# Lightning attention and a low-rank mixer on one core: low-rank rows through ScalarE, V converted a step sooner, and 64x64 score tiles from step nine

## The chip, the cores and the metric

The kernel runs on one core of a Trainium2 chip. The metric is the time of one execution in microseconds on the device. Eight runs of the kernel before took 674.75 to 678.09 us, with a median of 675.93. Five engines work side by side: TensorE (PE; its weight loads are listed apart as PEld), VectorE (DVE), ScalarE (ACT), GpSimd (POOL), and SyncE (SP), which only issues DMAs here. Matrix products land in PSUM, which VectorE and ScalarE read; everything else lies in SBUF.

## What is computed

The first half is attention with a decay per head, in 4 batches, 8 heads, 768 positions and head size 64. The second half mixes the positions through a rank of 32 and the channels through a layer of 2048:

```python
intra = np.einsum('bhic,bhjc->bhij', qb, kb) * Dmask[None]      # scores, masked by lam ** (i - j)
intra = np.einsum('bhij,bhjd->bhid', intra, vb)
inter = np.einsum('bhid,bhde->bhie', qb * lam_pow[None], kv_state)
out[:, :, sl] = intra + inter
kv_state = lam_block[None, :, None, None] * kv_state + np.einsum('bhsd,bhse->bhde', kb_dec, vb)
...
h = xt @ U @ V                                                   # xt: positions last, rank 32
u = x + h.transpose(0, 2, 1)
ch = np.maximum(u @ w_ch1, 0.0) @ w_ch2
return (u + ch).astype(np.float32)
```

U, V, w_ch1 and w_ch2 arrive as float64. The kernel reads them as pairs of 32-bit words and makes float32 of them with integer and float operations. The products of the second half run on a reduced float32 format. So an operand is split into a high part (its upper bits, by a mask) and a low part (the rest), and the products of the parts are added.

## The kernel before

**Steps.** The positions are cut into 24 steps of 128 (6 per batch, `NT`), and the first part of the kernel runs through them with an order that is written out by hand (lines 546 to 566; each engine takes its work in just this order). A step s turns q and k of step s+1 (`prep`, L348 on TensorE, copied out by ScalarE, L351), multiplies the masked scores by V (`intra`, L446), copies the result x to SBUF (L451, ScalarE), updates the state (`state`, L411 on TensorE and L417 or L419 on VectorE), makes the scores of the next step (`scores`, L393), multiplies q by the state (`inter`, L434), and masks the scores (`masked`, L402, VectorE). There are nine buffers for x. GpSimd scales k (L365) and q (L376). SyncE issues the loads of q, k and V three to five steps ahead (L272) and waits for buffers to come free in the order of its own queue.

**Scores.** For each of eight heads the scores are a product of k with 64 rows and q. For steps 0 to 11 it is one product with 128 columns of k (form 64x128); from step 12 on it is two products with 64 columns each, into the upper and the lower half of the output (form 64x64). L411, L434 and L446 have 64 output rows per product throughout.

**The low-rank stage.** When a batch's six x are there, `low` (L461) forms the 32 low-rank rows of the batch in PSUM, in four groups of 32 partitions (tile `pp`, in the bank with the tag `pq`, which the next q transposes also use). `low_rows` brings them to SBUF side by side, as 32 rows of 512, split: four VectorE masks out of PSUM (L474) make the high part `p_h`; four VectorE subtractions, also out of PSUM (L480), make the low part. ScalarE spreads the high part to two places (L485, L486) and copies the low part (L489). `next_of_low` issues these pieces in between other work. Then `mix` (L499) multiplies V's split by these rows, VectorE adds the result to x (L502), and `turn` (L516) transposes the sum, splits it (L521 and after) and stores it (L519). This store is what frees a buffer of x. For batches 0 to 2 the stage lies in steps 6, 12 and 18; for batch 3 it lies among the first products of the channel layer (`rest`, L769), where ScalarE also reads the products' results (L720).

**Side work.** The conversion of U, V and the first two tiles of w_ch1 is cut into pieces, which the table at L623 gives to steps; `aside` issues them at the end of a step, and what falls to ScalarE comes in the next step (`late`). V's pieces are two fetches, four pieces of conversion (L154 to L184, with L160 and L161 on ScalarE), the mask and first copies (L597, L604), the low part (L608 on VectorE and on GpSimd).

**After the steps** come the two channel products: `hidden` (L714, L724) makes u times w_ch1 with weights that are converted alongside and stores the result; `product` (L847, L849, L851) multiplies by w_ch2.

Of the kernel before, what the change touches and what calls it, by code (L numbers as in the profile page):

```python
# [10 lines left out]
U32 = mybir.dt.uint32  # L11
AF = mybir.ActivationFunctionType
ALU = mybir.AluOpType

P = 128
# [3 lines left out]
def kernel(  # L19
# [28 lines left out]
    nc = tc.nc  # L48
# [3 lines left out]
    NT = S // P  # L52
# [4 lines left out]
    R = moe_U.shape[1]  # L57
# [6 lines left out]
    HI = 0xFFFFF000  # L64
# [16 lines left out]
    def on_scalar(what):  # L81
        if late and late[0] is None:
            late.append(what)
        else:
            what()
# [12 lines left out]
    def tmp(name):  # L98
        return wconv.tile([P, C], FP32, tag="tmp", bufs=3, name=name)
# [125 lines left out]
    def w1_steps(ft, in_parts=False):  # L225
        def tile_of():
            w1v[ft] = w1_pool.tile([P, 3, C], F32R, tag="w1", name="w1")
            return w1v[ft]

        cols = moe_w_ch1[:, ft * P : (ft + 1) * P].rearrange("(c p) f -> p c f", p=P)  # L230
        return split_steps(tile_of, cols, in_parts)
# [13 lines left out]
    def two_banks(name, tag):  # L245
        return psf.tile([P, 2, N], FP32, tag=tag, name=name)

    def one_bank(shape, name, tag):
        return psf.tile(shape, FP32, tag=tag, name=name)
# [80 lines left out]
    half = [slice(0, D), slice(D, P)]  # L330

    def keep_busy(n):

        out = one_bank([P, C], "idle", "pq")
        for i in range(n):
            nc.tensor.matmul(out=out[:, 0:P], lhsT=blank, rhs=blank, start=True, stop=True)
# [50 lines left out]
    def scores(s):  # L387
        qt, kt = st[s]["qt"], st[s]["kt"]
        st[s]["pss"] = pss = two_banks("pss", "pss").rearrange("p x (a i) -> p x a i", a=HP)
        for a in range(HP):  # L390
            for x in range(2):
                for rows in half if s >= 2 * NT else [slice(0, P)]:
                    nc.tensor.matmul(  # L393
                        out=pss[rows, x, a, :], lhsT=kt[half[x], a, rows],
                        rhs=qt[half[x], a, :], start=True, stop=True,
                    )
# [57 lines left out]
    pps = {}  # L454
# [12 lines left out]

    def low_rows(b):

        pp, t = pps.pop(b), tmp("p_h")[0:R]  # L470
        h, h2, l, l2 = (p_hl[g * R : (g + 1) * R] for g in range(G))
        own = [(slice(g * R, (g + 1) * R), slice(g * P, (g + 1) * P)) for g in range(G)]
        for rows, cols in own:
            nc.vector.tensor_scalar(  # L474
                t[:, cols].bitcast(U32), pp[rows].bitcast(U32), HI, None, ALU.bitwise_and
            )

        def low_part():
            for rows, cols in own:
                nc.vector.tensor_tensor(  # L480
                    out=l[:, cols], in0=pp[rows], in1=t[:, cols], op=ALU.subtract
                )

        def spread():
            nc.scalar.copy(h, t)  # L485
            nc.scalar.copy(h2, t)  # L486

        def spread_low():
            nc.scalar.copy(l2, l.bitcast(FP32))  # L489

        pps[b] = [spread, low_part, spread_low]
# [55 lines left out]
    for s in range(NS):  # L547
        b, c = divmod(s, NT)
# [20 lines left out]
    def load_next(name, engine=nc.sync):  # L569
# [3 lines left out]

    run = {
        "prep": prep, "fade": fade, "scores": scores, "masked": masked, "inter": inter,
        "intra": intra, "state": state,
        "low": low, "low_rows": low_rows, "next_of_low": next_of_low, "mix": mix, "turn": turn,
        "scale": scale, "turned": lambda s: turned.pop(s)(),
    }
    def v_steps():  # L580

        st = {}

        def dst():
            if "v" not in st:
                st["v"] = wconv.tile([P, C], FP32, tag="wf", name="vf")[0 : 2 * R, 0:SH]
            return st["v"]

        def parts(gs):
            for half in range(2):  # L590
                rows, cols = slice(half * R, (half + 1) * R), slice(half * SH, (half + 1) * SH)
                for g in gs:
                    yield v_hl[g * R : (g + 1) * R, cols], rows

        def five():
            st["t"] = t = wconv.tile([P, C], FP32, tag="wt", name="vt")[0 : 2 * R, 0:SH]
            nc.vector.tensor_scalar(  # L597
                t.bitcast(U32), st["v"].bitcast(U32), HI, None, ALU.bitwise_and
            )
            on_scalar(lambda: high(0))  # L600

        def high(g, copy=nc.scalar.copy):
            for out, rows in parts((g,)):
                copy(out, st["t"][rows])  # L604

        def low(g, engine):
            for out, rows in parts((g,)):
                engine.tensor_tensor(  # L608
                    out=out, in0=st["v"][rows], in1=st["t"][rows], op=ALU.subtract
                )  # L610

        halves = [moe_V[:, half * SH : (half + 1) * SH] for half in range(2)]
        return weight_steps(dst, halves, SH, 2 * R, in_parts=True) + [
            five, lambda: low(1, nc.vector), lambda: high(2, nc.vector.tensor_copy),
            lambda: low(3, nc.gpsimd),
        ]
# [5 lines left out]
    side = {}  # L622
    for steps, at in (  # L623
        (u_side, (-1, 1, 1, 2, 2)),
        (v_steps(), (0, 0, 3, 3, 4, 4, 4, 5, 4, 5)),
        (w1_steps(0, True), (3, 4, 5, 6, 8, 9, 10, 11, 12, 13, 14)),
        (w1_steps(1, True), (8, 9, 10, 11, 15, 16, 17, 18, 19, 20, 21)),
    ):
        assert len(steps) == len(at)
        for step, n in zip(steps, at):  # L630
            side.setdefault(n, []).append(step)
# [28 lines left out]
    keep_busy(2)  # L660
    pl = one_bank([P, H], "pl", "pt")
    nc.tensor.matmul(out=pl, lhsT=lam_row[:, H:], rhs=lam_row[:, 0:H], start=True, stop=True)
    keep_busy(3)
    nc.vector.tensor_copy(out=lamb, in_=pl)
    constants()
    powers()
# [101 lines left out]
    c0, b = NS - NT, B - 1  # L768
# [181 lines left out]
```

## Time and profile before

| what | value |
|---|---|
| median of eight runs | 675.93 us (674.75 to 678.09) |
| the profiled execution | 678.09 us, its span 676.1 us |
| mean granted TensorE clock | 1.000 |
| TensorE busy | 666.7 us, 99% of the span |
| VectorE, ScalarE, GpSimd busy | 498.2, 277.5, 113.4 us |
| DMA | 131.27 MB, mean 194 GB/s |
| steps of the first part | from 4.5 to 125 us |
| channel layer | from 125 us to the end |
| L393 in form 64x128, in form 64x64 | 192 matmuls of 296 ns, 384 of 275 ns |
| L474, L480 (VectorE, 32x128) | 16 of 285 ns, 16 of 288 ns |
| L485, L486, L489 (ScalarE, 32x512) | 4 each of 617, 618, 616 ns |

In the timelines a line has the start in us from the beginning of the span, the duration in us, the engine, the line of the kernel, the operation, the tiles written and read, the shape and the count; in square brackets stands how long the engine was idle before, and who ended that. In the chain of waits a line has start, duration, and the engine and line, or the DMA, that the end of the kernel hung on at that time. In the list of groups, "busy, mean ns" are the total time and the mean duration of one instruction. A float32 matmul counts as two in the profile's counts, since the hardware runs it as two passes.

### The profile page before, as it was taken

The page shows a single profiled execution, that of the slowest core. Times are in us where ns is not written, and L with a number is a line of the kernel's source. Part 1 is how long each engine was busy: PE and PEld are TensorE (multiplying, and loading weights), DVE is VectorE, ACT ScalarE, POOL GpSimd, SP SyncE. Part 2 cuts the span into 40 slices and gives each one's busy share as a digit, 9 for nine tenths or more (in the row PEclk, how much of TensorE's full clock was granted, in tenths as well). Part 3 has the DMA queues.
Part 4 walks back from the last instruction along what each step waited for, and adds up shares of the span by engine and source line. Part 5 has one row for each costly group of instructions (what it writes and reads, how often), then busy time and mean ns, then how long its engine had stood idle before and what let it go on. Part 6 is the DMA issues. An engine that isn't in the chain of part 4 may idle for free.

```text
span 676.1 us, 13173 instructions
## 1 busy us (share of the span) xinstructions
PE 666.7 (99%) x5124; PEld 545.1 (81%) x5124; DVE 498.2 (74%) x879; ACT 277.5 (41%) x513; POOL 113.4 (17%) x92
## 2 busy tenths in 40 slices
PE   9998999999999999999999999999999999999997
PEld 7887888887888888888888888888888888888886
DVE  4678989777999777777798255786686776865864
ACT  4665658544555444444455122232232322322320
POOL 4455767331000000000000000030030210300300
PEclk9999999999999999999999999999999999999999
DMA  8888987164777655555667999844363353453431
GB/s 196 207 201 215 236 208 188 56 213 141 255 258 253 234 202 203 202 203 194 211 249 248 329 313 391 303 165 155 104 203 106 113 194 102 148 164 94 157 93 62
DMA packets 131775, 131.27 MB, mean 194 GB/s; under 512 B 81346, under 2 KB 89794, under 8 KB 131714
## 3 DMA queue, kind: packets, MB, share of 16 engines
q1 hardware_dynamic: 130656, 130.18, 61.2%
q8 instruction: 40, 0.66, 0.4%
q10 hardware_dynamic: 1058, 0.26, 0.2%
q14 instruction: 21, 0.17, 0.1%
HBM read 80.09 MB, written 50.33 MB: 193 GB/s over the span
## 4 chain that ended last, share of the span: by engine, by line
PE 94%; ACT 2%; DVE 2%; DMA 2%; issue 0%; DVEq 0%; ACTq 0%
PE pz L714 27%; PE pz L849 13%; PE pd L724 13%; PE pz L847 13%; PE pd L851 13%; PE px L446 3%; PE pss L393 3%; PE put L516 2%; PE pq L348 1%; PE pkv L411 1%; PE px L434 1%; PE pk L348 1%; DMA vraw<-in_v_dram 1%; DMA u_d<-x_nat 1%; PE pp L461 1%; PE pu L499 1%
## 5 line engine op out<-in xcount | busy, mean ns | idle before, releaser
L714 PE MATMUL pz<-u_hl,w 128*128 128x512 f32 x768 | 190.5, 397 | 0.0
L714 PEld LDWEIGHTS pz<-u_hl,w 128*128 128x128 f32 x768 | 144.0, 188 | 35.5 <-issue 0.4
L849 PE MATMUL pz<-w_hl,m 128*128 128x512 f32 x384 | 151.1, 396 | 0.0
L847 PE MATMUL pz<-w_hl,m 128*128 128x512 f32 x384 | 150.9, 396 | 0.0
L851 PE MATMUL pd<-w_d,m 128*128 128x512 f32 x384 | 149.5, 396 | 0.0
L830 ACT ACTIVATE m<-mt 128x512 fp32r<-128x512 f32 x96 | 60.7, 633 | 196.3 <-PE pd L851 130.0
L831 DVE SCALAR_TENSOR_TENSOR m<-rm,m 128x512 fp32r<-128x512 f32 x96 | 71.4, 745 | 45.5 <-ACT m L830 45.3
L876 POOL TENSOR_TENSOR o<-o,u 128x512 f32<-128x512 f32 x20 | 29.8, 1523 | 447.4 <-DVE o L872 447.4
L729 DVE SCALAR_TENSOR_TENSOR r<-pd,r 128x512 f32<-128x512 f32 x96 | 61.8, 686 | 53.6 <-ACT r L720 43.5
L724 PE MATMUL pd<-u_d,w 128*128 128x512 f32 x384 | 98.6, 397 | 0.0
L720 ACT ACTIVATE r<-pz 128x512 f32<-128x512 f32 x96 | 52.2, 596 | 93.4 <-PE pz L714 93.3
L849 PEld LDWEIGHTS pz<-w_hl,m 128*128 128x128 f32 x384 | 72.3, 188 | 17.7
L847 PEld LDWEIGHTS pz<-w_hl,m 128*128 128x128 f32 x384 | 72.3, 188 | 17.6
L851 PEld LDWEIGHTS pd<-w_d,m 128*128 128x128 f32 x384 | 72.3, 188 | 17.6
L724 PEld LDWEIGHTS pd<-u_d,w 128*128 128x128 f32 x384 | 72.1, 188 | 17.3
L829 DVE TENSOR_SCALAR mt<-rm 128x512 uint32<-128x512 uint32 x96 | 46.2, 482 | 34.9 <-DMA rm<-r_d 34.5
L832 DVE SCALAR_TENSOR_TENSOR m<-m 128x512 fp32r<-128x512 f32 x96 | 69.0, 720 | 0.9
L402 DVE TENSOR_TENSOR sm<-pss,mask 128x512 f32<-128x512 f32 x48 | 30.8, 684 | 6.7 <-PE pss L393 6.6
L205 ACT CAST w<-wt 128x512 fp32r<-128x512 f32 x32 | 19.9, 622 | 30.5 <-DVE wt L202 23.4
L446 PEld LDWEIGHTS px<-vraw,sm 128*64 128x64 f32 x768 | 25.0, 137 | 8.0 <-DVE sm L402 3.6
L446 PE MATMUL px<-vraw,sm 128*64 128x64 f32 x768 | 29.0, 226 | 1.9 <-DVE sm L402 0.8
L376 POOL TENSOR_TENSOR qs<-qt,powq 128x512 f32<-128x512 f32 x20 | 26.3, 1316 | 23.6 <-ACT qt L351 22.8
(85 smaller groups left out, 682.3 us busy)
## 6 DMA issues: line engine op xcount, KB each, us to landing
r_d<-r SPq DMA_DIRECT2D x96, 256.0 KB, 2.4
rm<-r_d SPq DMA_DIRECT2D x96, 256.0 KB, 2.8
words<-in_moe_w_ch_dram SPq DMA_DIRECT2D x30, 512.0 KB, 4.3
w_d<-w SPq DMA_DIRECT2D x16, 768.0 KB, 3.3
w_hl<-w_d SPq DMA_DIRECT2D x16, 512.0 KB, 6.5
vraw<-in_v_dram SPq DMA_DIRECT2D x24, 256.0 KB, 5.5
u_d<-x_nat SPq DMA_DIRECT2D x24, 256.0 KB, 4.0
u<-u_d SPq DMA_DIRECT2D x24, 256.0 KB, 4.1
```

Source lines behind the costliest of these rows:

```text
L446: nc.tensor.matmul(out=px[half[t], x, a, :], lhsT=sm[:, x, a, half[t]], rhs=vr[:, 2 * a + x, :], start=(first and a == 0), stop=(a == HP - 1),
L714: nc.tensor.matmul(out=acc[g][0], lhsT=w[:, n, ct, :], rhs=uhl[g][:, n, ct, :], start=(ct == 0 and n == 0), stop=(ct == CT - 1 and n == 1),)
L720: nc.scalar.mul(rs[g], acc[g][0], 4096.0 + 1.0)
L724: nc.tensor.matmul(out=acc[g][1], lhsT=w[:, 2, ct, :], rhs=ud[g][:, ct, :], start=(ct == 0), stop=(ct == CT - 1),)
L729: nc.vector.scalar_tensor_tensor(rs[g], acc[g][1], 4096.0, rs[g], ALU.mult, ALU.add)
L829: nc.vector.tensor_scalar(t.bitcast(U32), r.bitcast(U32), HI, None, ALU.bitwise_and)
L830: nc.scalar.activation(out=m[:, 0], in_=t, func=AF.Relu)
L831: nc.vector.scalar_tensor_tensor(m[:, 1], r, 0.0, hi, ALU.max, ALU.subtract)
L832: nc.vector.scalar_tensor_tensor(m[:, 2], hi, E, low, ALU.mult, ALU.subtract)
L847: nc.tensor.matmul(out=pz, lhsT=m[:, 0, cols], rhs=hl[:, 0], start=first, stop=False)
L849: nc.tensor.matmul(out=pz, lhsT=m[:, 1, cols], rhs=hl[:, 1], start=False, stop=end)
L851: nc.tensor.matmul(out=pd, lhsT=m[:, 2, cols], rhs=dd, start=first, stop=end)
```

## The change

Four edits, all in the part before the channel layer's long run. The scores take the 64x64 form from step 9 on, not from step 12 on. In `low_rows` four ScalarE copies bring the rows out of PSUM into a new SBUF tile `p_f` (from the same three rotating buffers as `p_h`); the mask and the subtraction are then one VectorE operation each, on 32x512, out of SBUF. V's conversion, though not its fetches, is given to steps 2 to 4, not 3 to 5. And one more idle matmul stands before the first transposes.

```diff
-                for rows in half if s >= 2 * NT else [slice(0, P)]:
+                for rows in half if s >= NT + 3 else [slice(0, P)]:
...
-        pp, t = pps.pop(b), tmp("p_h")[0:R]
+        pp, t, rows_f = pps.pop(b), tmp("p_h")[0:R], tmp("p_f")[0:R]
...
         for rows, cols in own:
-            nc.vector.tensor_scalar(
-                t[:, cols].bitcast(U32), pp[rows].bitcast(U32), HI, None, ALU.bitwise_and
-            )
+            nc.scalar.copy(rows_f[:, cols], pp[rows])
+        nc.vector.tensor_scalar(t.bitcast(U32), rows_f.bitcast(U32), HI, None, ALU.bitwise_and)
 
         def low_part():
-            for rows, cols in own:
-                nc.vector.tensor_tensor(
-                    out=l[:, cols], in0=pp[rows], in1=t[:, cols], op=ALU.subtract
-                )
+            nc.vector.tensor_tensor(out=l, in0=rows_f, in1=t, op=ALU.subtract)
...
-        (v_steps(), (0, 0, 3, 3, 4, 4, 4, 5, 4, 5)),
+        (v_steps(), (0, 0, 2, 2, 3, 3, 3, 4, 3, 4)),
...
-    keep_busy(3)
+    keep_busy(4)
```

On TensorE the order is the same but for the form of L393 in three steps and the idle matmul. On SyncE the order is the same. On VectorE and GpSimd V's pieces come one step sooner; on GpSimd V's two L608 now stand ahead of the L365 of step 7.

## The prediction

> **What bounds the kernel now.** First the page's opening and its chain of work.
>
> ```profile
> span 676.1 us, 13173 instructions
> PE 666.7 (99%) x5124; PEld 545.1 (81%) x5124; DVE 498.2 (74%) x879; ACT 277.5 (41%) x513; POOL 113.4 (17%) x92
> ...
> PE 94%; ACT 2%; DVE 2%; DMA 2%; issue 0%; DVEq 0%; ACTq 0%
> ```
>
> TensorE ends the kernel: 94% of the chain is its own work, and the mean granted clock is 1.000. From about 125 us on, the chain is TensorE without a break, so a microsecond lost or won there is one of the total. All that is edited lies before 134 us. Next, therefore, the same chain in order of time, cut to that part.
>
> ```profile
> 25.84 6.11 DMA vraw<-in_v_dram
> 31.94 0.14 issue
> 32.08 1.15 PE px L446 x32
> ...
> 40.49 0.31 DVE vp L480
> 40.80 0.04 issue
> 40.84 0.66 PE pq L348 x4
> ...
> 50.37 5.88 DMA u_d<-x_nat
> 56.25 0.02 issue
> ...
> 61.45 1.09 PE pss L393 x16
> 62.54 0.62 PE px L434 x32
> ```
>
> Twice the chain leaves the engines for a DMA. Step 5's intra product waits for V until 32.08 (TensorE idle 0.70 us); step 9's copy of x waits until 56.25 for the store of step 0's u, which frees its buffer (TensorE idle 0.94 us before L434). Between them stands the low-rank stage of batch 0, where VectorE's L474 and L480 hold the bank that the next transposes need. Last, the timelines of VectorE, GpSimd and ScalarE around the four low-rank stages. The first two lines below are VectorE's, the third is GpSimd's, the last four ScalarE's.
>
> ```profile
> 102.55 1.25 DVE L480 TENSOR_TENSOR vp<-pp,p_h 32x128 fp32r<-32x128 f32 x4
> 103.82 0.69 DVE L184 SCALAR_TENSOR_TENSOR wf<-m,sc 128x512 f32<-128x512 f32 x1
> ...
> 102.19 1.06 POOL L365 TENSOR_TENSOR ks<-kraw,small 128x512 f32<-128x512 f32 x1 [1.90 <-DVE p_h L474]
> ...
> 131.18 0.62 ACT L485 CAST vp<-p_h 32x512 fp32r<-32x512 f32 x1 [2.05 <-DVE p_h L474]
> 131.81 0.62 ACT L486 CAST vp<-p_h 32x512 fp32r<-32x512 f32 x1
> 132.46 0.62 ACT L489 CAST vp<-vp 32x512 fp32r<-32x512 f32 x1
> 133.10 1.09 ACT L720 ACTIVATE r<-pz 128x512 f32<-128x512 f32 x2
> ```
>
> The spread (L485, L486) and its low half (L489) end at 133.08; TensorE reaches the product that reads them, L499, at 133.24. That is 0.16 us of slack at the last place where a delay still counts in full.
>
> **Part 1, the scores of steps 9 to 11.** In the 64x128 form a step's scores take 1.09 us (61.45) and the L434 behind them 0.62 (62.54). From step 12 on, in the 64x64 form, the chain has 1.03 and 0.46 (77.17 and 78.20). So each of three steps saves 0.06 + 0.16 = 0.22, together 0.66 us. Steps 9 and 10 run into the wait that ends at 56.25 and into ScalarE's queue behind it (L451 at 56.33 to the copies that end at 60.72, with pkv waiting at 60.77), so their 0.44 is hidden in this execution. Step 11's 0.22 is not: TensorE leads from 60.77 to 68.
>
> **Part 2, V's conversion a step sooner.** Its two fetches stay in step 0, so SyncE's queue is unchanged; VectorE, ScalarE and GpSimd get the work earlier. The first block (L154, L155, L171: 0.34 + 0.34 + 0.55 = 1.2 us with spacing) moves from 26.69 to 23.14, behind U's L184. V's words landed at 22.66 by the landings of its two transfers, so it does not wait, and it ends at 24.4, just before the state update L419 at 24.46. The second block (L179, L184, L597, two L604: 30.98 to 33.95, 2.97 us) moves to 26.69 and ends at 29.66. Queued behind it are step 4's L419, now at 28.75, and the mask of step 5, now at 29.77. TensorE's L434 at 29.66 reads that state: it starts near 30.15, 0.5 us late. The cover is the 0.70 us in which TensorE waits for V at 32.08. On ScalarE L160 and L161 (1.24 us) move to step 3 ahead of a 0.76 us gap and a copy at 26.74, late by some 0.1. On GpSimd the two L608 pass ahead of one L365, which is needed only at 43.5. What it buys is at 35.69: VectorE's two L608 (2.10 us) leave the stretch between the mask of step 6 and L474.
>
> **Part 3, one more idle matmul.** The three before the first transposes take 1.58 us, 0.53 each. TensorE then runs without a wait to 6.68, so up to 0.53 is added; as the transposes get faster from 5.8 on (0.66 to 0.43 us for a pair), I take 0.3. This too ends in the wait at 32.08. With part 2's 0.5 it comes to 0.8 against a cover of 0.70, so some 0.1 is left over there, and all 0.8 if that wait were gone.
>
> **Part 4, the low-rank rows.** Per batch VectorE loses four L474 (1.23 us) and four L480 (1.25) that read PSUM. It gets one 32x512 mask and one 32x512 subtraction out of SBUF. ScalarE gets four copies of 32x128 out of PSUM. No row shows such a copy. Copies out of PSUM take 590 ns for 512 columns and 373 for 256, which extrapolates to 265 for 128; the shortest ScalarE row of the head is 338 for 64 columns. Four in a row take 0.76 us if they overlap as the others do (each starts 0.1 before the last has ended), 1.35 us if they are as long as the latter and do not. I take 0.9.
> - Batches 0 to 2: ScalarE sits idle until the intra product is done (2.21 us, to 38.29, 71.37 and 101.62), and pp is ready 1.1 to 1.2 us before that. The copies fit; at 1.35 they would cost 0.2 each.
> - The mask from SBUF: L202 has 442 ns for 128x512. It replaces 1.23 us, but what follows it, L417, waits for TensorE's pkv anyway.
> - The subtraction: 685 ns is the nearest row (L210 into fp32), 1.3 us its other end: the same line into fp32r at 77.63 and 112.62 took 1.29 and 1.30, both times beside GpSimd's L365. Here L365 (102.19 to 103.25; 38.80 and 71.94 before) starts with L417 and covers the subtraction's place. I take 1.3: no gain over the 1.25 of four L480 in batches 1 and 2, rather 0.1 lost in each; 0.5 would be won in each at 0.69. In batch 1 ScalarE's copies end at 76.44, when pkv starts, so a faster VectorE is worth nothing there.
> - Batch 0: TensorE's transposes need not wait for L480 (0.42 us idle at 40.84), since the bank is free after the copies, near 38.0. The mask of step 7 and L489 come 0.25 us sooner with a subtraction of 1.3, 0.6 with 0.69. I take 0.25 because of the same row.
> - Batch 3: pp is done at 129.72; the copies end near 130.7, the mask at 131.2, the spread starts at 131.2 to 131.3 against 131.18. TensorE's slack of 0.16 holds up to 0.9 us of copies. Counted as 0.
>
> [...]
>
> **Sum.** In this execution: step 11 -0.22, batches 1 and 2 +0.2, batch 3 0; all before 57 us (+0.3 +0.5 -0.25 -0.44) is hidden by two DMA waits. That is 0 against the execution's own time of 678.09 (span 676.1 and 2.0 around it). The median of the eight runs is 675.93, 2.2 lower, and the two DMA stalls are the likeliest thing to be shorter there. Then about half of the 0.69 that parts 1 and 4 save before 57 us comes through: -0.3. **Forecast: 675.93 - 0.3 = 675.6**, own range 674.9 to 676.3.
>
> **Rivals.**
> - A, the second DMA wait is peculiar to this execution and GpSimd does not hold the subtraction up: 0.66 of scores, 0.6 in batch 0, 0.3 in batch 2, with parts 2 and 3 still hidden: -1.6, 674.3. For it: the profiled run is the slowest of eight. Against: SyncE's queue. The V load at 52.82 took 3.25 us to issue, though its buffer was free since 49.2, so DMA sets that pace and not TensorE.
> - B, slower: V's words land too late for their new place. L154 stands in VectorE's queue ahead of L419 (24.46) and the mask of step 4. The words landed 0.5 us before they will be asked for, 3.8 us after their second issue at 18.83; loads of V take 4.4 to 6.4. At 6.4 they land at 25.2: VectorE loses 2.0 us, TensorE's L434 (25.36) waits 1.5. This decides from a landing at 23.2 on, and once the loss passes the 0.70 us of cover. With the leftover of part 3, +1.2: 677.1.
> - C, nothing arrives: each saving ends in a DMA wait or behind ScalarE: 675.9.
>
> **How the numbers follow.** Forecast 0.48, A 0.28, B 0.15, C 0.09. A measurement can tell about 0.2%, 1.35 us, from no change. A lies 0.2 beyond that: 0.22 of its 0.28 and 0.02 of the forecast are "faster"; half of B, which lies 0.2 short of it, is "slower", 0.08; the rest is "same". The range takes in A and B with 0.3 around them, 674.0 to 677.3.
>
> **What would show it.** Right: L434 in steps 9 to 11 at 0.46, the copies inside ScalarE's gap before L451, a subtraction near 1.3 beside L365, L419 of step 4 near 29.7, L499 of step 18 without a wait. Wrong: a subtraction of 0.7, no DMA wait near 56 (A); VectorE waiting for V's words near 23 (B); ScalarE's copies over 0.9 in all, with TensorE idle at 133.

## The result: 0.55% slower

The changed kernel takes 679.89 us in the median (678.18 to 681.75, 12 runs) against 675.95 us before (35 runs of the kernel before on the same chip): a ratio of 1.0055, 95% interval 1.0045 to 1.0065. The prediction had 675.6 us with a range of 674.0 to 677.3. It was wrong in sign as well as in size.

The profiled execution took 678.92 us. In the changed kernel, lines from `low_rows` on have numbers lower by 4: V's mask is L593, the casts L600, V's low part L604, `mix` L495. First the page, the opening and the chain by engine.

```profile
span 677.1 us, 13262 instructions
PE 666.1 (98%) x5174; PEld 545.3 (81%) x5174; DVE 498.3 (74%) x855; ACT 281.6 (42%) x529; POOL 113.4 (17%) x92
...
PE 94%; DVE 3%; ACT 2%; issue 1%; DVEq 0%; ACTq 0%
```

TensorE has less work than before (666.1 us for 666.7), and the span is longer. The DMAs have left the chain, and VectorE has 3% of it for 2%. A percent of this span is 6.8 us, so the next place to look is the stretch in which VectorE got work: V's conversion, 22 to 32 us. VectorE's timeline, the changed kernel (start, duration, engine, line, operation, tiles, shapes, count, idle time before it):

```profile
22.82 1.43 DVE L154 TENSOR_SCALAR sc<-words 64x384 uint32<-64x384 uint32 x1
...
25.03 0.41 DVE L419 TENSOR_TENSOR kv<-pkv,faded 128x256 f32<-128x256 f32 x1
...
27.72 1.40 DVE L593 TENSOR_SCALAR vt<-vf 64x384 uint32<-64x384 uint32 x1
29.14 2.16 DVE L600 CAST vp<-vt 32x384 fp32r<-32x384 f32 x2
31.34 0.42 DVE L419 TENSOR_TENSOR kv<-pkv,faded 128x256 f32<-128x256 f32 x1
```

GpSimd's timeline of the same stretch:

```profile
22.76 1.28 POOL L376 TENSOR_TENSOR qs<-qt,powq 128x512 f32<-128x512 f32 x1 [1.85 <-ACT qt L351]
27.62 1.28 POOL L376 TENSOR_TENSOR qs<-qt,powq 128x512 f32<-128x512 f32 x1 [3.59 <-ACT qt L351]
28.86 1.17 POOL L365 TENSOR_TENSOR ks<-kraw,small 128x512 f32<-128x512 f32 x1
```

And TensorE's:

```profile
28.78 1.16 PE L393 MATMUL pss<-qt,kt 64*128 64x128 f32 x16
31.91 0.69 PE L434 MATMUL px<-kv,qs 64*64 64x64 f32 x32 [1.97 <-DVE kv L419]
```

Read the three together. In the kernel before, the same block stood some 4 us later, with L154 and the mask clear of GpSimd's work. VectorE's rows first, then GpSimd's, then TensorE's, all of the kernel before:

```profile
26.69 0.34 DVE L154 TENSOR_SCALAR sc<-words 64x384 uint32<-64x384 uint32 x1
...
32.14 0.35 DVE L597 TENSOR_SCALAR vt<-vf 64x384 uint32<-64x384 uint32 x1
32.52 1.43 DVE L604 CAST vp<-vt 32x384 fp32r<-32x384 f32 x2
...
27.40 1.61 POOL L376 TENSOR_TENSOR qs<-qt,powq 128x512 f32<-128x512 f32 x1 [3.01 <-ACT qt L351]
28.98 2.07 POOL L365 TENSOR_TENSOR ks<-kraw,small 128x512 f32<-128x512 f32 x2
...
29.66 0.69 PE L434 MATMUL px<-kv,qs 64*64 64x64 f32 x32
```

L154 and the mask (L593) are 64x384 operations that took 0.34 and 0.35 us in the kernel before. Here they take 1.43 and 1.40, and both end 0.2 us after the GpSimd operation that was under way when they began (24.04 and 28.90). The two casts took 1.43 us and take 2.16. Between them, the chain of waits shows 1.07 us from 29.18 on in which VectorE waited for nothing that the profile names; GpSimd's L365 ends at 30.03. So step 4's state update L419, queued behind them, starts at 31.34 and not near 29.7, and TensorE stands idle for 1.97 us ahead of L434. Before, L434 ran at 29.66 without a wait.

The second thing that is new is further on, in TensorE's timeline:

```profile
77.40 0.51 PE L434 MATMUL px<-kv,qs 64*64 64x64 f32 x18
78.92 0.46 PE L434 MATMUL px<-kv,qs 64*64 64x64 f32 x14 [1.01 <-issue]
...
104.65 0.34 PE L434 MATMUL px<-kv,qs 64*64 64x64 f32 x7 [0.72 <-issue]
```

TensorE stops in the middle of a row of equal products, with the state and q long there, for 1.01 and 0.72 us. No wait that the profile shows ends these stops ("issue").

The third is in the runs' clocks. Six of the changed kernel's 13 executions have a mean granted clock of 0.997, the others 0.999 or 1.000. Of the kernel before, 137 executions beside the later runs have their clock on record: 1.000 or 0.999, but for one.

### The profile page after: what moved, and what is told of

The parts are those of the page before. It is cut to its first block, busy times and chain, and to the rows that moved or that the text cites. A ratio compares the mean times of both kernels' runs of the same rounds, so it can differ in the third digit from the quotient of the medians.

```text
span 677.1 us, 13262 instructions
## 1 busy us (share of the span) xinstructions
PE 666.1 (98%) x5174; PEld 545.3 (81%) x5174; DVE 498.3 (74%) x855; ACT 281.6 (42%) x529; POOL 113.4 (17%) x92
## 4 chain that ended last, share of the span: by engine, by line
PE 94%; DVE 3%; ACT 2%; issue 1%; DVEq 0%; ACTq 0%
PE pz L710 27%; PE pz L843 13%; PE pz L845 13%; PE pd L720 13%; PE pd L847 13%; PE pss L393 3%; PE px L446 3%; PE put L512 2%; PE pq L348 1%; PE px L434 1%; PE pkv L411 1%; PE pk L348 1%; PE pp L461 1%; DVE sm L402 1%; PE pu L495 1%
## 5 line engine op out<-in xcount | busy, mean ns | idle before, releaser
L376 POOL TENSOR_TENSOR qs<-qt,powq 128x512 f32<-128x512 f32 x20 | 25.6, 1282 | 27.1 <-ACT qt L351 26.8
L446 PEld LDWEIGHTS px<-vraw,sm 128*64 128x64 f32 x768 | 24.6, 137 | 6.3 <-issue 2.3
L446 PE MATMUL px<-vraw,sm 128*64 128x64 f32 x768 | 28.2, 226 | 0.7 <-DVE sm L402 0.6
```

The costliest lines, as they stand in the source:

```text
L446: nc.tensor.matmul(out=px[half[t], x, a, :], lhsT=sm[:, x, a, half[t]], rhs=vr[:, 2 * a + x, :], start=(first and a == 0), stop=(a == HP - 1),
```

## Theories

**Theory 1:** the loss is V's second block. It stands ahead of step 4's L419 and GpSimd holds it up; TensorE's wait of 2 us then halves its clock for a while in some executions. **Theory 2:** the other three edits make the loss, by late fetches of TensorE's instructions above all. **Theory 3** in the first group of runs: the low-rank rows make it. That fell at once. From v_scores on, the expectations give its number to a new theory, grown out of Theory 2: stops at fixed places of TensorE's instruction stream, brought by the scores edit.

## The experiments

All were timed in five rounds beside the kernel before. A ratio is the recorded one, with its 95% interval; it is not the quotient of the two medians and can differ from it by 0.1% (as for p_scores below). Each run has a short name, such as p_v, in brackets. Where two medians of one kernel are given, its executions are parted by the clock.

### One edit alone

Each of the four edits was put into the kernel before by itself. V's move (p_v):

```diff
-        (v_steps(), (0, 0, 3, 3, 4, 4, 4, 5, 4, 5)),
+        (v_steps(), (0, 0, 2, 2, 3, 3, 3, 4, 3, 4)),
```

> The kernel before with V's conversion a step sooner, nothing else. Theory 1 (VectorE's block is held up by GpSimd in its new place, as the profile after shows with L154 at 1.43 and L593 at 1.40 us, and delays the state of step 5 by over 2 us): +1.5 to +3.5 us, and the late V load at 32 us covers at most 0.7 of it. Theory 2 (instruction fetches of TensorE): 0. Theory 3 (the low-rank rows): 0.

Measured: 678.15 us against 676.09, ratio 1.0031 (1.0018 to 1.0044). One execution of 1085.06 us, with a mean clock of 0.559, is left out. The scores edit (p_scores):

```diff
-                for rows in half if s >= 2 * NT else [slice(0, P)]:
+                for rows in half if s >= NT + 3 else [slice(0, P)]:
```

> The kernel before with the 64x64 scores from step 9 on, nothing else. Theory 1: -0.7 to 0 us, as on record (0.22 a step, of which two steps may be hidden). Theory 2 (24 more matmuls in the stretch where TensorE's instructions come late through busy DMA engines): +1 to +3. Theory 3: -0.7 to 0.

Measured: 675.51, ratio 1.0005 (0.9992 to 1.0018). The low-rank rows (p_rows):

```diff
+            nc.scalar.copy(rows_f[:, cols], pp[rows])
+        nc.vector.tensor_scalar(t.bitcast(U32), rows_f.bitcast(U32), HI, None, ALU.bitwise_and)
...
+            nc.vector.tensor_tensor(out=l, in0=rows_f, in1=t, op=ALU.subtract)
```

> The kernel before with the low-rank rows through ScalarE, nothing else. Theory 1: -0.5 to +0.3 us. Theory 2: 0. Theory 3 (the subtraction out of SBUF waits for GpSimd in each batch, and the four copies, 1.07 us, delay ScalarE in each): +1 to +3.

Measured: 675.54, ratio 0.9996 (0.9983 to 1.001). The idle matmul (p_keep):

```diff
-    keep_busy(3)
+    keep_busy(4)
```

> The kernel before with a fourth idle matmul, nothing else. On record was +0.3, hidden later. The profile after shows step 1's scores 0.36 us sooner with it, so I now expect -0.4 to +0.2 under all theories.

Measured: 675.52, ratio 0.9999 (0.9987 to 1.001). Of the four, V's move is the only one whose cost is clear of the intervals. It costs 2.1 us, and the four together cost 3.9.

### One edit taken back

The same four, taken out of the changed kernel one at a time (the last three in 5 or 6 executions each). V back in its old steps (u_v):

```diff
-        (v_steps(), (0, 0, 2, 2, 3, 3, 3, 4, 3, 4)),
+        (v_steps(), (0, 0, 3, 3, 4, 4, 4, 5, 4, 5)),
```

> The changed kernel with V's conversion back in its old steps. Theory 1 (V's place alone costs, held up by GpSimd; a TensorE idle of 2 us near 30 us then also halves its clock for 3.4 us in some executions; the other three edits cost nothing by themselves): 674.5 to 676.2 us, no slower than before, no halved clock. Theory 2 (the other three edits together cost what V alone, +2.1 us, does not explain): 677 to 678.5.

Measured: 675.86 against 675.56, ratio 1.0004 (0.9994 to 1.0014). The scores back (u_scores):

```diff
-                for rows in half if s >= NT + 3 else [slice(0, P)]:
+                for rows in half if s >= 2 * NT else [slice(0, P)]:
```

> The changed kernel with the scores of steps 9 to 11 back on 64x128. Theory 1: 679 to 680.6 us, as the changed kernel or up to 0.7 more. Theory 2, if the scores are the part that costs (a fetch of TensorE's instructions that comes late, 1.0 us at 77.9 in the profile after): 677.5 to 678.5.

Measured: 677.43, ratio 1.0038 (1.0024 to 1.0052). The low-rank rows back (u_rows):

```diff
-            nc.scalar.copy(rows_f[:, cols], pp[rows])
+            nc.vector.tensor_scalar(
+                t[:, cols].bitcast(U32), pp[rows].bitcast(U32), HI, None, ALU.bitwise_and
+            )
...
```

> The changed kernel with the low-rank rows on VectorE again. Theory 1: 679 to 680.5 us, as the changed kernel. Theory 2, if the rows are the part that costs once VectorE is late: 677.5 to 678.5.

Measured: 678.86, ratio 1.0050 (1.0037 to 1.0063). The idle matmul back (u_keep):

```diff
-    keep_busy(4)
+    keep_busy(3)
```

> The changed kernel with three idle matmuls. Theory 1: the matmul moves the start of step 0 and with it the time of the TensorE idle near 30 us by some 0.3 us, which may decide in how many executions the clock is halved: 678 to 680. Theory 2: 679.9, no change.

Measured: 677.95, ratio 1.0046 (1.003 to 1.0062). Without V's move the loss is gone; without any other edit most of it stays. So V's move is needed for the loss. What the others add to it is left for the last group; there it is the scores.

### What in V's move costs

**The first block alone** (e_first). Only the first four conversion pieces come a step sooner:

```diff
-        (v_steps(), (0, 0, 3, 3, 4, 4, 4, 5, 4, 5)),
+        (v_steps(), (0, 0, 2, 2, 4, 4, 4, 5, 4, 5)),
```

> The kernel before, with only V's first four conversion pieces a step sooner (the first block: L154, L155, L171 in step 2); the second block (L179, L184, mask, casts) stays in its old place. Theory 1 (the loss comes from the second block, which stands ahead of step 4's L419 and is held up by GpSimd): the first block is held up by GpSimd's L376 too (L154 1.4 us in place of 0.34), so L419 of step 3 comes 0.6 us late and TensorE waits 0.5 us once; that ends in the wait for V's load near 32 and the median is 675.9 to 676.5, no run with a clock of 0.997. If instead the first block or the earlier use of V's words makes the loss: 677 or more.

Measured: 675.95 against 675.45, ratio 1.0007 (0.9998 to 1.0016). The first block is not the loss, though GpSimd holds L154 up here just as much. VectorE's timeline in that kernel:

```profile
22.94 1.43 DVE L154 TENSOR_SCALAR sc<-words 64x384 uint32<-64x384 uint32 x1
...
25.15 0.41 DVE L419 TENSOR_TENSOR kv<-pkv,faded 128x256 f32<-128x256 f32 x1
```

L419 came at 24.46 in the kernel before. It is 0.7 us late, TensorE waits 0.51 us once, and no more follows.

**The casts off VectorE** (e_casts), in the changed kernel. ScalarE makes them:

```diff
-            five, lambda: low(1, nc.vector), lambda: high(2, nc.vector.tensor_copy),
+            five, lambda: low(1, nc.vector), lambda: on_scalar(lambda: high(2)),
```

> The changed kernel, with the two casts of V's second half (2.16 us on VectorE, ahead of step 4's L419) given to ScalarE behind the two that it makes already. Theory 1: L419 starts near 29.2 where it started at 31.34, TensorE's idle ahead of L434 falls from 1.97 us to under 0.3, no run has the clock of 0.997, and the median is 675.7 to 676.7 against 679.9 for the changed kernel. ScalarE then works until some 31.2 and the copy of the next q may come up to 1 us late: then 677. If the loss does not come from this wait (late instruction fetches of TensorE, the other edits): 678.5 or more.

Measured: 676.18, ratio 1.0009 (1.0 to 1.0017). Its profile, VectorE's timeline:

```profile
27.73 1.39 DVE L593 TENSOR_SCALAR vt<-vf 64x384 uint32<-64x384 uint32 x1
29.04 0.41 DVE L419 TENSOR_TENSOR kv<-pkv,faded 128x256 f32<-128x256 f32 x1
```

and TensorE's:

```profile
29.88 0.69 PE L434 MATMUL px<-kv,qs 64*64 64x64 f32 x32
```

The mask is still held up (1.39 us), but with the casts gone L419 comes at 29.04 and L434 does not wait. Of 3.9 us, 0.7 is left, with all four edits in place.

**GpSimd kept out** (e_lock), with V's move alone. VectorE's block has the same instructions in the same place:

```diff
+            if s != 5:
+                st[s]["qs"] = qs = att.tile([P, HP, P], FP32, tag="qs", bufs=2, name="qs")
+                nc.gpsimd.tensor_tensor(out=qs, in0=st[s]["qt"], in1=powq, op=ALU.mult)
+            else:
+                st[s]["qs"] = st[s]["qt"]
+        if s + 1 < NS and s not in (5, 6):
...
+            (nc.vector if s in (6, 7) else nc.gpsimd).tensor_tensor(
...
-            lambda: low(3, nc.gpsimd),
+            lambda: low(3, nc.vector),
...
+        if s in (4, 5):
+            scale_k(s + 2)
```

> V's conversion a step sooner alone, with GpSimd kept out of the stretch: step 5's q is not scaled (that product uses q as it is, so the output is another), the scaled k of steps 6 and 7 and V's last low part are made by VectorE, all behind the mask of step 5. VectorE's second block has the same instructions in the same place as with V's move alone. Theory 1, GpSimd holds the block up: the mask (1.39 us) is back at 0.35, the two casts (2.17) at 1.43, the block ends near 29.7 where it ended at 31.6, L434 waits some 0.4 us and not 1.96, no clock of 0.997, median 675.5 to 676.5; VectorE's added 2.7 us lie between 31 and 38, where it sat idle 1.6 us, and may give 0.5 back. If the block is as long without GpSimd: 678.

Measured: 675.56, ratio 1.0003 (0.9993 to 1.0012). VectorE's timeline (lines there are 3 higher than in the kernel before: L600 is the mask, L607 the casts, L422 the state update):

```profile
27.96 0.35 DVE L600 TENSOR_SCALAR vt<-vf 64x384 uint32<-64x384 uint32 x1
28.34 0.72 DVE L607 CAST vp<-vt 32x384 fp32r<-32x384 f32 x2
29.37 0.42 DVE L422 TENSOR_TENSOR kv<-pkv,faded 128x256 f32<-128x256 f32 x1 [0.31 <-PE pkv L414]
```

The mask is back at 0.35 us and the two casts together take 0.72, half of the 1.43 that they took even in the kernel before (there GpSimd's L608 started beside them at 32.63). L422 now waits for TensorE instead of for its own queue. Same instructions, same order, no GpSimd: no loss. Theory 1 holds for V's move. The figure that I had taken for an undisturbed block, 2.97 us, was itself disturbed.

### The clock behind the wait

In the profile of V's move alone the clock record has half speed from 32.30 to 35.72 us, 3.41 us, starting 0.12 us after L434 starts behind its wait. TensorE's timeline:

```profile
32.18 1.07 PE L434 MATMUL px<-kv,qs 64*64 64x64 f32 x32 [1.96 <-DVE kv L419]
33.18 1.11 PE L348 MATMUL pq<-ident,qraw 128*128 128x128 f32 x4
34.09 1.06 PE L348 MATMUL pk<-ident,kraw 128*128 128x128 f32 x4
```

Stretches of the same profile (length, busy time and instructions of PE, PEld, DVE, ACT and POOL, granted clock, DMA share, GB/s):

```profile
28.00:32.00 4.00, 2.21 (x56) 1.95 (x50) 3.92 (x5) 1.91 (x4) 3.86 (x4) 1.00 1.01 227
32.00:36.00 4.00, 3.82 (x62) 3.40 (x64) 2.49 (x5) 1.17 (x2) 1.49 (x2) 0.57 1.03 243
```

The granted clock is 0.57 in the second row. The groups take 1.06 to 1.11 us in place of 0.60 to 0.69. A mean clock of 0.997 is what 3.41 us at half speed give over 669 us. By that mark, 24 of 64 executions of the seven kernels with a long wait ahead of L434 had it (the changed kernel 6 of 13, p_v 4 of 11, u_scores 2 of 6, u_rows 2 of 5, u_keep 1 of 6, v_scores 5 of 12, one of them at 0.996, a_sc7 4 of 11), and none of 116 of the ten kernels without one and without a filler. Beside them the kernel before had it once in 137.

The profiles also suggest which executions are hit. In p_v, full speed lasts 23.89 us before the slow stretch, seven times the 3.41 us of that stretch. From these two lengths I estimate that the clock record changes on a grid of 3.41 us. Two of the seven profiles halved, p_v and u_scores. There TensorE is busy for 1.45 and 1.46 us in the 3.41 us that end where the half speed begins (28.89 to 32.30 and 29.32 to 32.74). In the five that kept their clock, no stretch of that grid around the wait has less than 1.71 us (u_rows, 28.69 to 32.11). So how the wait falls on such a grid may decide; no run tests it.

To show that the idle time is the cause, it was filled. First with V's move alone (e_fill):

```diff
+        if s == 5:
+            keep_busy(8)
         for a in range(HP):
```

> V's conversion a step sooner alone, and eight idle matmuls on TensorE just ahead of step 5's L434, in the place where TensorE waits 1.96 us for the state. They take some 1.7 us by the rows of the start once the clock is full, so L434 starts when it did. If the idle time is what halves the clock from 32 us on in about half of the executions: no run has a clock of 0.997 and the median is 677.1, the median of those runs of V's move alone that kept their clock (all its runs: 678.15). If the lower clock has another cause: again 4 in 10 runs at 0.997 and 678.2. If the fill is longer than I count (0.53 each): 679.

Measured: 678.15, ratio 1.0032 (1.0021 to 1.0044), six executions, none with 0.997. (One has a clock record of 0.948 over its whole span, with a time like the others'.) The filler took 2.06 us, as long as the wait. The median did not fall to 677.1 as expected; six executions say little. Then in the changed kernel, one matmul fewer (a_fill):

```diff
+        if s == 5:
+            keep_busy(7)
         for a in range(HP):
```

> The changed kernel with seven idle matmuls ahead of step 5's L434, which fill 1.8 of the 1.97 us of TensorE's wait (eight took 2.06 us and were 0.27 too long). If the wait is what halves the clock: no run with the clock of 0.997 (the changed kernel had 6 of 13), and a median of 678.9, that of the changed kernel's runs which kept their clock, against 679.9. If not: 5 or 6 of 12 runs at 0.997 and 679.9.

Measured: 678.02, ratio 1.0026 (1.0011 to 1.004), 12 executions, none with 0.997. TensorE's timeline:

```profile
29.70 1.83 PE L336 MATMUL idle<-blank 128*128 128x128 f32 x14
31.75 0.69 PE L436 MATMUL px<-kv,qs 64*64 64x64 f32 x32 [0.21 <-DVE kv L419]
```

The state comes as late as ever and the clock stays. In 18 filled executions there was no halving. At 24 in 64 the chance of that is 0.02%, so the wait is the cause. The price is read from kernels whose executions part by the clock: p_v 677.1 and 679.0, v_scores 677.9 and 679.7, a_sc7 676.6 and 678.6, the changed kernel 678.9 and 680.0. That is 1.1 to 2.1 us in those executions. The fall of 1.9 us in a_fill's median is not all the clock's: the 14 passes of the filler also move the stops of the next group.

### What the other edits add

**V and scores together** (v_scores):

```diff
+                for rows in half if s >= NT + 3 else [slice(0, P)]:
...
+        (v_steps(), (0, 0, 2, 2, 3, 3, 3, 4, 3, 4)),
```

> V's conversion a step sooner and the scores of steps 9 to 11 in 64x64 tiles, nothing else changed. V's move alone gave a ratio of 1.0031 and the four edits together 1.0055. Theory 3, the scores edit brings stalls of TensorE ahead of L434 that no wait explains (the profiles of the kernels with this edit all have them, 0.4 to 1.7 us in all, those without it have none), and behind the delay of step 5 they are not hidden: ratio 1.004 to 1.005, 679.0, with such stalls between 60 and 105 us. Rival: the two edits' prices add (-0.2 for the scores): 1.003, 678.0, and the rest of the loss is the low-rank rows' or the idle matmul's.

Measured: 678.53 against 676.20, ratio 1.0034 (1.0018 to 1.0051). The stops were there (0.29, 0.57 and 0.40 us), the extra loss was not. The interval reaches both cases, so this run decided nothing.

**64x64 from step 6 on** (scores6), in the kernel before:

```diff
-                for rows in half if s >= 2 * NT else [slice(0, P)]:
+                for rows in half if s >= NT else [slice(0, P)]:
```

> The kernel before with 64x64 tiles from step 6 on instead of step 12. By the prediction's own price of 0.22 us a step this takes 1.3 us off TensorE's path, of which steps 6 to 10 may be hidden by the wait for the store near 56: 674.8 to 675.6. Theory 3, more products in smaller tiles bring stalls ahead of L434 that no wait explains: they come to 0.4 us or more in all, some of them already before 60 us, and the median is 675.5 to 676.5, no faster than before.

Measured: 676.18, ratio 0.9994 (0.9979 to 1.0009). It has more small products than any kernel so far and not one stop in L434. Theory 3, as it was put in that expectation, was wrong: the form does not bring the stops.

**GpSimd kept out of the changed kernel** (a_lock: the edit of e_lock, on all four edits):

```diff
+        if s + 1 < NS and s not in (5, 6):
...
+            (nc.vector if s in (6, 7) else nc.gpsimd).tensor_tensor(
...
```

> The changed kernel with GpSimd kept out of VectorE's second block in the same way as with V's move alone: step 5's q is not scaled (its product uses q as it is, so the output is another), the scaled k of steps 6 and 7 and V's last low part are VectorE's. All four edits and V's early place stay. Theory 1, the changed kernel's loss is V's second block held up by GpSimd: L434 of step 5 waits under 0.5 us, no clock of 0.997, median 675.5 to 676.5. If the edits together cost something beyond this wait: 677 or more.

Measured: 677.43, ratio 1.0019 (0.9999 to 1.0039). L434 of step 5 does not wait and no execution has 0.997, so some 2 us of the loss are gone. What remains has, in the profile, stops of 1.28, 0.79 and 0.34 us in L434, and one wait of 1.00 us for GpSimd's L365 at 61.57, which this experiment may have made itself. ScalarE also waits three times for a store of u, for 2.0 to 2.5 us (54.41, 60.88 and 66.48). The expectation missed by 1 us.

**Where the stops sit.** Numbering TensorE's matmul records (passes) from the start, all stops in the middle of L434 of over 0.1 us and later than 30 us come ahead of the passes 1228, 1480, 1607, 1733, 2239 or 2366, within one, in nine kernels and at times that differ by 1.4 to 3.4 us for the same pass. One more, of 0.49 us in u_v, sits ahead of pass 344, seven gaps of 126.5 before 1228 within two. The gaps between these numbers are multiples of 126.5. With one weight load to each pass (5174 of each) that is 253 instructions, and with the 116 waits in 5174 passes, 2.8 more: some 256, an estimate from these counts. The page of the changed kernel shows how instructions arrive:

```profile
q8 instruction: 41, 0.67, 0.4%
```

41 packets, 0.67 MB: 16 KB each. TensorE's 10348 matmul and load records and 116 waits make 40.9 blocks of 256, for 41 packets. The traces show stops at the borders of such blocks of up to 1.35 us (u_rows).

A step with 64x64 tiles has 125 passes here (32 each in L393, L434 and L446, 16 in L411, 8 in L348, 5 in L512 and L495), a block 126.5. So a border stays in the same line step after step. In the kernels with 64x64 from step 9 it falls mostly into L434, whose 32 passes take 0.64 to 0.69 us where L446 takes 1.15: the fastest use of instructions in a step. In the kernels with it from step 12 the same passes lie in L446, and with it from step 6 in L393. None of those stops there (the one stop at a border outside L434 is 0.14 us, in the L446 of the kernel before, ahead of pass 1858). Nor does every border in L434 stop: of the 9 to 11 from pass 1228 on, 1 to 3 do in any one profile of the nine.

What ends a stop is in the packed traces, which have the times of queue 8's packets, one ahead of each border. Each of the 21 stops ends 1.2 to 1.6 us after such a packet has landed, whether the stop is 0.1 or 1.35 us long (the three of the changed kernel's profile, at passes 1480, 1607 and 2239, 1.40, 1.42 and 1.40 us after packets that landed at 71.07, 77.50 and 103.26). In the two kernels with 64x64 from step 7 (below), TensorE reaches the borders between passes 1228 and 2745 1.5 to 4.2 us after the landing, and does not stop in L434. So, by these times, TensorE waits in the stops for its next block of instructions, which lands late.

Filling with seven matmuls moved the stop of a_fill 14 passes ahead in its L434 (21 passes left behind it, 7 in the changed kernel), again at pass 2239. Hence the last two runs, which move the borders by putting two more steps on small tiles: 64x64 from step 7, 32 passes more. In the changed kernel (a_sc7):

```diff
-                for rows in half if s >= NT + 3 else [slice(0, P)]:
+                for rows in half if s >= NT + 1 else [slice(0, P)]:
```

> The changed kernel with the 64x64 scores from step 7 on instead of step 9: 32 more matmul passes before step 9, so everything behind stands 32 passes later in TensorE's stream of instructions. Theory 3: the unexplained stalls of the profiles sit ahead of the same numbers of that stream (passes 1228, 1480, 1607, 1733, 2239, 2366, each within one, multiples of some 126.5 apart), whatever the time, and stop TensorE only where these fall into L434, the line that uses up instructions fastest; here they fall into L393 and there is no such stall. Two steps more save 0.22 each, mostly hidden. Ratio 1.002 to 1.0045 (677.5 to 679.0) against 1.0055, since V's late block and the halved clock stay. If the stalls belong to the 64x64 form itself, or to the time: some of 0.4 us or more again, and 679.5 or more.

Measured: 677.28 against 675.23, ratio 1.0030 (1.0019 to 1.0041). And with V back in its old steps as well (u_v_sc7):

```diff
-                for rows in half if s >= NT + 3 else [slice(0, P)]:
+                for rows in half if s >= NT + 1 else [slice(0, P)]:
...
-        (v_steps(), (0, 0, 2, 2, 3, 3, 3, 4, 3, 4)),
+        (v_steps(), (0, 0, 3, 3, 4, 4, 4, 5, 4, 5)),
```

> The changed kernel with V's conversion back in its old steps and the 64x64 scores from step 7 on. With V back alone, the profile had 1.71 us of unexplained stalls in L434 and the median was that of the kernel before (1.0004). Theory 3: here these stalls are gone and five steps save 0.22 each, of which those from step 10 on count: ratio 0.998 to 0.9995, 674.6 to 675.6, the first version that would beat the kernel before, though by less than the interval may show. If the stalls come again or were hidden anyway: 1.000 to 1.001.

Measured: 674.18 against 675.23, ratio 0.9989 (0.998 to 0.9999). TensorE's timeline of u_v, with V back but 64x64 from step 9:

```profile
70.89 0.41 PE L434 MATMUL px<-kv,qs 64*64 64x64 f32 x16
71.96 0.46 PE L434 MATMUL px<-kv,qs 64*64 64x64 f32 x16 [0.67 <-issue]
76.52 0.51 PE L434 MATMUL px<-kv,qs 64*64 64x64 f32 x18
77.91 0.46 PE L434 MATMUL px<-kv,qs 64*64 64x64 f32 x14 [0.89 <-issue]
```

and of u_v_sc7:

```profile
68.65 0.64 PE L434 MATMUL px<-kv,qs 64*64 64x64 f32 x32
74.11 0.64 PE L434 MATMUL px<-kv,qs 64*64 64x64 f32 x32
```

No stop in L434 is left in either new profile. The changed kernel drops from 1.0055 to 1.0030, with intervals that do not touch: 1.7 us, of which two more steps of small tiles can explain 0.44 at most by the prediction's own 0.22 each. With V back the drop is from 1.0004 to 0.9989, 1.0 us, with intervals that just overlap. u_v_sc7 is the one version that beats the kernel before, by 0.1%; its interval just leaves out 1.

**The account of the 3.9 us:** 1.0 for V's late block by itself (p_v's executions that kept their clock), 1.0 for the halved clock (the changed kernel's median against that of its executions that kept the clock, 679.89 and 678.92), and 1.3 to 1.7 for the stops. That makes 3.3 to 3.7; the rest is within the intervals. What was not settled is why some blocks land late and others in time; that busy DMA engines delay them, as Theory 2 had it in p_scores' expectation, no run shows. And why V and scores together measured no more than V alone stays open within their intervals.

## Why the prediction was wrong, point by point

**Part 2 is the step that failed**, in its second block. "30.98 to 33.95, 2.97 us" was moved to 26.69 and "ends at 29.66": the durations were carried to a place where GpSimd works from 27.62 to 30.03. The block ended at 31.30, which delayed L434 by 2.25 us, not 0.5. Its first block, too, took 2.3 us and not 1.2. The cover, the 0.70 us of the V load at 32.08, belonged to one execution: in none of the 19 other profiles does TensorE wait for step 5's V, also where V's conversion stands in its old steps. How much of the 2.25 us other waits covered is not known; 1.0 us came through in p_v's executions that kept their clock. A sign of this stood in the prediction itself, under Part 4: the slow rows of L210, 1.29 and 1.30 us, both beside GpSimd's L365. The runs agree: the mask takes 0.35 us without GpSimd (e_lock) and 1.39 to 1.40 beside it (e_casts, the changed kernel). I weighed such a delay for one operation of 1.3 us and did not ask about it for the eight that Part 2 moved. GpSimd's L376 at 27.40 and L365 at 28.98 were in the trace of before (rows above).

**What the wait does to the clock** was not in the sum at all. In 24 of 64 executions the clock halved, and where the price could be read the loss is 1.1 to 2.1 us larger for it.

**Part 1** had the saving right where nothing stops (scores6's chain has 1.03 and 0.46 us for a step's scores and L434, at 60.85 and 61.89) and left out that more instructions move the block borders into L434. Alone, the scores edit shows no gain: 1.0005, with an interval from 0.9992, where 0.66 us would be 0.9990. Its profile has one stop of 0.40 us.

**Part 3**: p_keep shows no cost. The 0.3 us that I took were hidden or not there; the first scores of the changed kernel's profile end 0.36 us sooner instead, in an execution whose full clock begins at 7.40 us and not at 8.32.

**Part 4 had its durations right.** ScalarE's copies and VectorE's mask and subtraction in the changed kernel (batch 0), with the beginning of GpSimd's L365 at 40.27:

```profile
39.80 0.41 DVE L475 TENSOR_SCALAR p_h<-p_f 32x512 uint32<-32x512 uint32 x1 [2.66 <-ACT p_f L474]
...
40.69 1.19 DVE L478 TENSOR_TENSOR vp<-p_f,p_h 32x512 fp32r<-32x512 f32 x1
```

The mask took 0.41 (442 ns predicted), the subtraction beside GpSimd 1.19 (1.3 predicted), the four copies 1.07 (0.9). In batches 1 and 2 the subtraction took 1.25 beside L365; in batch 3, with GpSimd idle, 0.68. There the last place with slack held, with 0.06 us left of 0.16: L495 follows TensorE's own work at 134.22 without a wait. p_rows measured 0.9996.

**Sum and rivals.** All before 57 us, the prediction said, is hidden by two DMA waits. The first, TensorE's for step 5's V, is in the profile of before alone, and the second, ScalarE's for the store of u, is there and in two of the 19 others, v_scores (2.01 us at 66.91) and a_lock. A sum for the median can't lean on them. So the first half of Rival A's condition was right for most profiles; the second, that GpSimd does not hold the subtraction up, was wrong: it took 1.19 to 1.25 us beside L365 and 0.68 without. No run shows the 0.3 us that A took for batch 2. That u_v_sc7 took 674.18, near A's 674.3, is luck: it is another kernel, and by its ratio it won 0.7 us, not 1.6. Rival B looked for the loss ahead of L419 too, but in the first block and in late words: the words had landed, since L154 starts at 22.82 without a wait, and the first block alone measured 1.0007. No rival named GpSimd beside V's block, and the range (B's 677.1 and 0.3 are 677.4, not 677.3) ended 2.6 us below the result.

## What to carry to other kernels

A duration belongs to the place where it was measured: before a VectorE block is moved, lay GpSimd's timeline under the new place, and look for a measured row of each operation with GpSimd beside it. Here a mask of 64x384 went from 0.35 us to 1.40, two casts from 0.72 to 2.16, a subtraction out of SBUF from 0.68 to 1.25. A wait of TensorE of some 2 us cost 1.1 to 2.1 us more than itself here, where the clock halved behind it. In unrolled code, instructions that an edit adds move all that follows along the instruction stream: here 32 passes more, ahead of borders that lie 126.5 passes apart, left no stop in L434 (a_sc7, u_v_sc7). When a neutral edit loses time in stops that nothing ends, count passes between them and look when the instruction queue's packets landed, here 1.2 to 1.6 us before the end of each stop.

## What the hardware showed beyond that

- The clock record halved for 3.41 us after a wait of some 2 us, in 24 of 64 executions by their mean clock. In p_v's profile it followed 1.96 us of idle time, with TensorE busy for 1.45 of the 3.41 us before.
- Idle matmuls held the clock: seven of them, 1.83 us, left 0 of 12 executions halved (a_fill); without them it was 6 of 13.
- Two casts of 32x384 took 0.72 us on VectorE without GpSimd (e_lock), 1.43 with its V work beside them (the kernel before), 2.16 between its L365 and its V work (the changed kernel).
